# A fused attention and feed-forward kernel: 7 block products for tile 2 of the second layer, and tile 1 in the written order

## The chip, the cores and the metric

The kernel runs on one core of one Trainium2 chip. The metric is the device time of one launch in microseconds (us). The core has five engines that run side by side, each through its own queue in order: PE (TensorE, matmuls, with its weight loads as PEld), DVE (VectorE), ACT (ScalarE), POOL (GpSimd) and SP (SyncE, which here only issues transfers). PE writes to PSUM, of which this kernel uses eight banks of 2 KB per partition.

## The reference

Attention with separate softmaxes, for 8 batches of 8 heads, 576 positions and 64 channels, and then a feed-forward block on the 4608 x 512 result:

```python
q_s = softmax(q, axis=-1)                      # over the channels of a head
k_s = softmax(k, axis=2)                       # over the positions
kv  = einsum('bhsd,bhse->bhde', k_s, v)        # 64 x 64 per head
x   = einsum('bhsd,bhde->bhse', q_s, kv)       # then to (4608, 512)
h   = x @ w_in                                 # 512 -> 2048
out = maximum(0.01 * h, h) @ w_out             # 2048 -> 512
```

## The kernel before

**Tiles and batches.** The feed-forward block works on 9 tiles (0 to 8) of 512 rows. The attention works on 8 batches of 576 rows, so tile t needs rows of one or two batches: tile 1 the last 64 rows of batch 0 (their first layer is made with tile 0 and carried over) and the first 448 of batch 1, tile 2 the last 128 of batch 1 and the first 384 rows of batch 2, tile 3 the rest of batch 2 and the start of batch 3. While PE works on tile t, the other engines prepare the batch that a later tile needs.

**One batch.** k, q and v are loaded whole (1152 KB each, `load`, L76) into one of six buffers (`raw_pool`, bufs=6), a buffer being given on when its last reader is done. For k: a tree of maxima on DVE (`k_tree`, four steps kt.0 to kt.3), the maximum over all partitions (`k_allmax`, km), subtraction (`k_sub`, ks and ksB for the halves on DVE, or one step on POOL), exponential on ACT (`k_exp`, ke). For v: a cast to bf16 in two halves (`v_cast`, va and vb). For q: maximum on DVE (`q_max`, qm), subtraction on POOL (`q_sub`, qs), exponential on ACT (`q_exp`, qe), sum and reciprocal on DVE (`q_sum`, qu), scaling on DVE (`q_norm`, qn), and a transposition by a DMA that SP issues (`q_turn`, qt; the result is the tile qX). Then 72 small matmuls make the key-value products (`kv`, into two PSUM banks), these are divided by the sums of the keys (`kd_make`, L308, on DVE: reciprocal and multiplication, twice), and `attend_made` (A.0, A.1, A.2 in words) multiplies qX by them; the results go from PSUM to the tile xT by copies (x words, on ACT).

**One tile.** The first layer is 16 blocks of 4 matmuls of 128x128 weights by 512 columns (`layer1`, words u) into PSUM, each followed by a leaky rectifier on ACT (`leaky`, words l). The plain second layer is, for each of four groups of 128 rows, 16 matmuls of 512 columns into one bank (`layer2`, words P with two digits: group, quarter) and a copy out (words d0 to d3). From tile 3 on the second layer goes by 7 block products in Strassen's manner instead of 8 (`behind`, words P with three digits: product, group, half): each product is 16 matmuls of 256 columns, on sums of weight blocks (`wsums`, words T, made once) and differences of the rectified blocks (words n, on DVE); what stands in PSUM between products is kept by ACT (words q1, q5, q6, q21) and totalled by DVE (words d11, d12, d22). Tiles 7 and 8, and tile 6 in part, do the same with the first layer too (`ahead`, words m, s, c; the sums F1 to F4 of the first layer's weights are made for them by `fsums`).

**The order.** The scheduler leaves the program's order as it is, so every engine works through its part of one written list. Tiles 0 and 1 are loops over the 16 blocks and the 4 groups of rows, with hooks: `at(t, u, ...)` puts steps at a place u of tile t, and `run(t, u)` calls them (L510 to L517). Tile 1's loop is L1051 to L1064; its hooks are `plan2` and `plan3` (L614 to L637). From tile 2 on the order is a string of words, `SCORE` (L775), which `play` (L1042) reads word by word: a word with a leading digit is of that tile (`of_tile`, L914), the others are of a batch (`of_batch`, L985): `lk3` loads k of batch 3, `kt4.0` is the first step of batch 4's tree. `KS_DVE` (L718) lists the batches whose k is subtracted on DVE.

**SP's queue** around the change issues, in program order: tile 0's 8 stores, the loads k, q, v of batch 3 (`load_all(3)` at place 2 of tile 1), the two halves of batch 2's transposition (places 16 and 17), tile 1's stores, with the loads of batch 4 between them (place 30), and then what SCORE says.

**PE's order in tile 1** is: 16 blocks of the first layer; the second layer's first two groups of rows (32 matmuls); kv of batch 2; the third group and a quarter of the fourth (20 matmuls); the first part of batch 2's attention (5 of 9 columns of positions), 8 matmuls, the second part, 4 matmuls; then tile 2's first layer.

## Time and profile before

| what | us |
|---|---|
| median of 3 runs (271.74 to 271.83) | 271.76 |
| the profiled execution | 271.57 |
| its span, first to last instruction | 269.8 |
| PE busy in the span | 261.4 (97%) |
| DVE busy | 222.3 (82%) |
| ACT busy | 182.4 (68%) |
| POOL busy | 65.1 (24%) |
| granted clock of PE | 1.0 |

A busy PE is not a PE at its peak, because matmuls overlap: one of 512 columns is shown with 379 ns, while in a run of them one starts every 216 ns. So spans of PE work are read from the chain of work that ended last, which gives start, length and count of merged pieces. For the other engines the groups by line and shape give the mean time of one instruction: 602 ns for a leaky step of 512 columns on ACT, 419 ns for a difference (L954) and 687 ns for a total (L852) on DVE, 2.55 us for the maximum or the scaling of a whole q on DVE, 2.14 us for its exponential on ACT, 4.43 us for its subtraction on POOL, 1.36 us for half a k's subtraction on DVE, 292 and 163 ns for the two steps of `kd_make`. Tile 1 runs from 49.9 to 77.9 us, tile 2 from there to 107.2.

### The profile page before, as it was taken

The numbers are of one execution on the slowest core, as the hardware profiler recorded it, in microseconds if no ns is written. First come the engines' busy times: TensorE is split into PE (matmuls) and PEld (weight loads), VectorE is DVE, ScalarE is ACT, GpSimd is POOL, SyncE is SP. The second block draws the span as 40 slices with busy tenths as digits, with TensorE's granted clock in tenths as the row PEclk, the third lists the DMA queues.
The fourth block names the chain that finished last, engine by engine and source line by source line (L and its number), as shares of the span: only waits on it lengthen the run. The fifth ranks groups of instructions, "written<-read, shape, count | busy, mean of one in ns | idle before, by whom it ended". The sixth has DMA issues, their size and how long they took to land.

```text
span 269.8 us, 6101 instructions
## 1 busy us (share of the span) xinstructions
PE 261.4 (97%) x2474; PEld 179.2 (66%) x2474; DVE 222.3 (82%) x391; ACT 182.4 (68%) x328; POOL 65.1 (24%) x46
## 2 busy tenths in 40 slices
PE   8799999999999999999999999999999999999993
PEld 3267744454444444447888884488888888888882
DVE  2997888896897998999599869985999679769953
ACT  4977890578468846857587287839997579628930
POOL 2584351009007700001920290029000000000000
PEclk9999999999999999999999999999999999999999
DMA  7999996999999645079299609900393060024004
GB/s 247 337 211 367 306 204 103 383 326 389 175 248 400 227 87 177 0 161 365 75 318 305 149 5 286 229 0 2 75 183 70 2 156 2 0 59 99 4 0 156
DMA packets 37900, 46.46 MB, mean 172 GB/s; under 512 B 18160, under 2 KB 21232, under 8 KB 37872
## 3 DMA queue, kind: packets, MB, share of 16 engines
q1 hardware_dynamic: 33504, 37.82, 48.5%
q0 software_dynamic: 4048, 7.73, 12.1%
q10 hardware_dynamic: 320, 0.52, 0.6%
q8 instruction: 19, 0.31, 0.5%
q14 instruction: 9, 0.07, 0.1%
HBM read 36.70 MB, written 9.44 MB: 171 GB/s over the span
## 4 chain that ended last, share of the span: by engine, by line
PE 88%; DMA 5%; DVE 1%; issue 0%; POOL 0%; ACT 0%; POOLq 0%
PE ph L474 29%; PE acc L903 27%; PE pout L499 14%; PE ph L873 14%; DMA w_in_sb<-in_moe_w_in_dram 3%; PE po L419 2%; DMA qX<-qe 2%; PE pkv L294 2%; DVE k_raw L361 1%; POOL w_in_sb L129 0%; DVE out_sb L852 0%; ACT out_sb L493 0%; POOL gate L558 0%; POOLq L558 0%
## 5 line engine op out<-in xcount | busy, mean ns | idle before, releaser
L474 PE MATMUL ph<-xT,w_in_sb 128*128 128x256 bf16 (+3 forms) x512 | 86.0, 326 | 0.3 <-DMA w_in_sb<-in_moe_w_in_dram 0.2
L483 ACT ACTIVATE gj<-ph 128x512 bf16<-128x512 f32 (+2 forms) x116 | 61.6, 572 | 18.6 <-PE ph L474 15.9
L474 PEld LDWEIGHTS <-w_in_sb 128*128 128x128 bf16 x512 | 49.6, 98 | 33.7 <-issue 0.9
L499 PE MATMUL pout<-w_out_sb,gj 128*128 128x512 bf16 x192 | 43.1, 379 | 0.0
L256 POOL TENSOR_TENSOR q_raw<-q_raw,qmax 128x2304 f32<-128x2304 f32 (+3 forms) x10 | 31.6, 3165 | 38.9 <-DVE qmax L225 38.9
L903 PEld LDWEIGHTS <-gs 128*128 128x128 bf16 x384 | 37.0, 98 | 5.5 <-issue 0.8
L499 PEld LDWEIGHTS <-gj 128*128 128x128 bf16 x192 | 18.2, 98 | 22.0 <-issue 1.1
L193 POOL TENSOR_TENSOR k_raw<-k_raw,kall 128x2304 f32<-128x2304 f32 x3 | 15.4, 5137 | 68.5 <-DVE kall L185 51.5
L903 PEld LDWEIGHTS <-gj 128*128 128x128 bf16 x288 | 28.1, 98 | 3.9 <-issue 0.2
L410 ACT CAST xT<-po 128x320 bf16<-128x320 f32 (+2 forms) x45 | 18.5, 486 | 15.4 <-PE po L419 15.4
L852 DVE TENSOR_TENSOR part_spare<-ph,part_spare 128x512 f32<-128x512 f32 x36 | 23.7, 685 | 2.8 <-PE ph L873 2.5
L936 ACT COPY part_spare<-ph 128x512 f32<-128x512 f32 x36 | 19.3, 593 | 8.1 <-PE ph L873 7.8
L903 PE MATMUL acc<-w_out_sb,gj 128*128 128x256 bf16 x192 | 23.7, 273 | 0.0
L273 DVE TENSOR_REDUCE qsum<-qe 128x36 f32<-128x2304 bf16 (+4 forms) x11 | 19.7, 1794 | 4.6 <-ACT qe L264 4.6
L903 PE MATMUL acc<-wsum,gs 128*128 128x256 bf16 x192 | 23.3, 273 | 0.0
L903 PE MATMUL acc<-w_out_sb,gs 128*128 128x256 bf16 x192 | 22.3, 273 | 0.0
L280 DVE TENSOR_TENSOR qe<-qe,qrec 128x2304 bf16<-128x2304 bf16 (+4 forms) x12 | 21.9, 1826 | 0.4
L852 DVE TENSOR_TENSOR out_sb<-acc,keep 128x512 f32<-128x512 f32 (+1 forms) x20 | 12.5, 635 | 11.6 <-ACT xT L410 4.9
L225 DVE TENSOR_REDUCE qmax<-q_raw 128x36 f32<-128x2304 f32 (+4 forms) x11 | 19.6, 1794 | 2.2 <-DMA q_raw<-in_q_dram 2.2
L873 PEld LDWEIGHTS <-fs_spare 128*128 128x128 bf16 x192 | 18.8, 98 | 2.2
L954 DVE TENSOR_TENSOR gs<-gj,gs 128x512 bf16<-128x512 bf16 x48 | 19.5, 419 | 0.9
L954 DVE TENSOR_TENSOR gs<-gj 128x512 bf16<-128x512 bf16 x48 | 19.0, 419 | 0.9 <-ACT gj L483 0.8
(89 smaller groups left out, 324.0 us busy)
## 6 DMA issues: line engine op xcount, KB each, us to landing
out_dram<-out_sb SPq DMA_DIRECT2D x68, 128.0 KB, 2.5
k_raw<-in_k_dram SPq DMA_DIRECT2D x6, 1152.0 KB, 6.9
q_raw<-in_q_dram SPq DMA_DIRECT2D x6, 1152.0 KB, 7.2
...
```

Source lines behind the costliest of these rows:

```text
L225: nc.vector.tensor_reduce(out=m, in_=st[b]["q"][:, :, rs], axis=AX.X, op=ALU.max)
L256: eng.tensor_tensor(out=qs, in0=qs, in1=st[b]["qmax", rs.start].unsqueeze(3).to_broadcast([P, HL, n, D]), op=ALU.subtract,)
L273: nc.vector.reduce_sum(out=qsum, in_=st[b]["qe"][:, rs], axis=AX.X)
L280: nc.vector.tensor_tensor(out=qes, in0=qes, in1=st[b]["qrec", rs.start].unsqueeze(3).to_broadcast([P, n, HL, D]), op=ALU.mult,)
L474: nc.tensor.matmul(ph[:, n0:n1], lhsT=w_in_sb[:, i, j * P : (j + 1) * P], rhs=xT[:, i, (c0 + n0) % NX : (c0 + n0) % NX + n1 - n0], start=( ...
L483: nc.scalar.activation(out=o, in_=ph, func=AF.Prelu, alpha=LEAKY_SLOPE)
L499: nc.tensor.matmul(pout, lhsT=g_at(g_sb, j, tsub * P, (tsub + 1) * P), rhs=w_out_sb[:, j], start=first, stop=last,)
L852: nc.vector.tensor_tensor(out=o, in0=x, in1=y, op=ALU.add)
L873: nc.tensor.matmul(bank[x, t, p][:, jj], lhsT=lhs(k, 2 * p + jj), rhs=rhs[:, k], start=(first and k == 0 and jj == 0), stop=(k == 1), skip ...
L903: nc.tensor.matmul(b[:, at_], lhsT=lhs(k)[:, sub * P : (sub + 1) * P], rhs=rhs[:, k], start=(first and k == 0 and at_ == 0), stop=(k % (NK ...
L936: nc.scalar.copy(out=fill(t, kind, p), in_=bank["Z" if kind == "s5" else "X", t, p])
L954: nc.vector.tensor_tensor(out=nt[t, p, i], in0=x, in1=y, op=ALU.subtract)
```

## The change

Four things are done together.

1. Tile 2's second layer goes by the 7 block products too (words `2P100` to `2P711`, `2n`, `2q`, `2d11`, `2d12`, `2d22` in place of `2P00` to `2P33` and `2d0` to `2d3`). The weight sums T4 and T3 are therefore made in tile 2, T3 after tile 1's last plain product; the sums F1, F2 and F3 of the first layer's weights move from tile 2 into tiles 3 and 4.
2. Tile 1 and batch 2 become words of `SCORE`; the loop of tile 1 and `plan2`, `plan3` go. PE's order in tile 1 stays nearly the same (kv of batch 2 after the second group of rows, its first attention words after a quarter of the fourth group), only the second part of its attention comes half a group earlier. Batch 2's q is one piece in every step, its v is cast on ACT in place of POOL, and the loads come in another order: `lk3 lq4 lq3 lv3` before batch 2's transposition `qt2`, then `lq5 lv5 lk4 lv4 lk5`.
3. For batches 2 to 7 the division of the key-value products is split: `kr` makes both reciprocals on DVE, `kd` scales on ACT by four activations of 128x64 (`kd_scale`).
4. The rest of `SCORE` (tiles 3 to 6) is another order of the same words. Two options (`QS_DVE`, `QN_POOL`) are added and left empty.

```diff
+    def kd_recs(b):
+        st[b]["krec"] = []
+        for hh in range(2):
+            krec = small_pool.tile([P, 2, 1], FP32, name="krec")
+            nc.vector.reciprocal(out=krec, in_=st[b]["pkv"][hh][:, :, D : D + 1])
+            st[b]["krec"].append(krec)
+
+    def kd_scale(b):
+        for hh in range(2):
+            for i in range(2):
+                nc.scalar.activation(
+                    out=kd2[b % 2][:, 2 * hh + i],
+                    in_=st[b]["pkv"][hh][:, i, 0:D],
+                    func=AF.Copy,
+                    scale=st[b]["krec"][hh][:, i],
+                )
...
-    at(1, 2, lambda: load_all(3))
-    at(1, 30, lambda: load_all(4))
...
-    plan2()
-    plan3()
...
-    WOVEN, KS_DVE = 7, (3, 4)
+    WOVEN = 7
+    KS_DVE, QS_DVE, QN_POOL, KD_ACT = (2, 3, 4), (), (), (2, 3, 4, 5, 6, 7)
...
     SCORE = """
-        2u00 2u04 2l04 2u01 2l00 2l01 km3 ks3 2u02 2u03 2l02 2l03 qm3 2u06 2l06 2u13 2u17 2l13 ksB3 ke3 2l17
...
+        lk3 1u04 1l04 lq4 1u00 1u06 1l06 1l00 1u02 1u07 1l07 1l02 1u03 1u12 1l12 kt2.0 kt2.1 1l03 kt2.2 1u14
+        1l14 1u13 qm2 kt2.3 1u10 1l10 1l13 1u15 qs2 1u11 1l11 1u05 1l05 1u01 1l01 km2 1u16 1l15 qe2 1P00
+        1u17 ks2 1l17 1l16 va2 ksB2 qu2 qn2 1P01 1P02 1P03 1P10 1P11 lq3 1P12 kt3.0 lv3 1P13 ke2 vb2 kv2
+        kt3.1 kr2 1d0 1d1 kd2 qt2 1P20 1P21 1P22 kt3.2 kt3.3 1P23 1P30 A2.0 x2.01 x2.00 lq5 qm3 A2.1 A2.2
+        x2.20 1P31 1P32 x2.21 x2.11 qm4 km3 qs3 1d2 1P33 x2.10 2u04 2u02 1d3 qe3 lv5 2l04 2u15 2l15 qu3 2l02
+        qn3 qs4 va3 2u00 2l00 1w0 2u01 2l01 2u10 lk4 2u11 2u03 2u13 2l10 2l03 2u12 2l12 2P100 2l11 2l13 2u05
+        2l05 2n2_0 2u14 2l14 T4 2u06 2u16 2n0_0 1w1 2n1_0 2n0_1 vb3 ks3 2u17 2l06 2u07 2n1_1 2n2_1 2P200
+        2l16 2l17 ksB3 kt4.0 2l07 2P201 2n3_1 2n0_2 2n0_3 2n1_3 2P210 2P101 2P110 2P111 2P211 2P500 qt3
+        2n1_2 2n3_2 ke3 kv3 2q1 2P600 2P501 qe4 2d11 2n2_3 2P601 2P610 2P611 2n3_3 kr3 2P510 2n2_2 kd3 kt4.1
+        T3 A3.0 2q6 lv4 2n3_0 A3.1 x3.10 A3.2 x3.01 2P511 2P700 2P701 2P710 2P711 x3.00 kt4.2 kt4.3 km4 2q5
+        2P300 2P301 lk5 2d22 qu4 qn4 qt4 2P310 2P311 2d12 x3.20 x3.21 x3.11 3u06 2P400 2P401 ks4 2P410 va4
+        vb4 2P411 2q21 3l06 3u00 3l00 ksB4 3u04 3u10 3l10 3u05 3u17 3l04 3l05 kt5.0 2w0 3u02 3l02 lv6 3l17
...
-    t, c0 = 1, L
-    for u, j in enumerate(ORDER):
-        ph = psB_pool.tile([P, TT - c0], FP32, name="ph", tag=BANK_TAG)
-        layer1(j, ph, t * TT + c0, TT - c0)
-        leaky(g_at(g_next, j, c0, TT), ph)
-        run(t, u)
-    for tsub in range(NTS):
...
     play(SCORE)
```

More of the change, by code (lines that the diff above doesn't have):

```diff
@@ L275, in q_sum, with q_norm @@
         nc.vector.reciprocal(out=qrec, in_=qsum)
-    def q_norm(b, rs):
+    def q_norm(b, rs, eng=nc.vector):
         n = rs.stop - rs.start
         qes = st[b]["qe"][:, rs]
-        nc.vector.tensor_tensor(
+        eng.tensor_tensor(
             out=qes,
@@ L609 @@
         at(0, (45, 46)[i], lambda i=i: attend_x(1, (i,), (nc.scalar, nc.vector)))
-    at(1, 2, lambda: load_all(3))
-    at(1, 30, lambda: load_all(4))
-    def plan3():
-        b, t = 3, 1
-        at(t, 27, lambda: k_begin(b), lambda: k_tree(b, ALLH))
-        at(t, 26, lambda: v_cast(nc.scalar, b, 0), lambda: v_cast(nc.scalar, b, 1))
-    def plan2():
-        b = 2
-        at(1, 0, lambda: k_begin(b), lambda: q_begin(b), lambda: k_tree(b, ALLH))
-        at(1, 3, lambda: k_allmax(b))
-        at(1, 6, lambda: k_sub(nc.vector, b, H0), lambda: k_sub(nc.vector, b, H1))
-        at(1, 12, lambda: k_exp(b, ALLH))
-        for rs in XR:
-            at(1, 9, lambda rs=rs: q_max(b, rs), lambda rs=rs: q_sub(nc.gpsimd, b, rs))
-        at(1, 13, lambda: v_cast(nc.gpsimd, b, 0), lambda: v_cast(nc.gpsimd, b, 1))
-        for i, rs in enumerate(XR):
-            at(1, (15, 16)[i], lambda rs=rs: q_exp(b, rs), lambda rs=rs: q_sum(b, rs), lambda rs=rs: q_norm(b, rs))
-            at(1, (16, 17)[i], lambda rs=rs: q_turn(b, rs))
-        at(1, 23, lambda: kv(b))
-        at(1, 24, lambda: kd_make(b))
-        for i in range(2):
-            at(1, 28 + 2 * i, lambda i=i: attend_x(b, (i,), (nc.scalar,)))
-    plan2()
-    plan3()
     W11, W12 = w_out_sb[:, 0:NK, 0:HO], w_out_sb[:, 0:NK, HO:O]
@@ L775 @@
     SCORE = """
-        2u00 2u04 2l04 2u01 2l00 2l01 km3 ks3 2u02 2u03 2l02 2l03 qm3 2u06 2l06 2u13 2u17 2l13 ksB3 ke3 2l17
-        2u16 2l16 2u11 2l11 2u10 2l10 qm4 qs3 F3 kv3 kd3 2u07 2u05 lk5 qe3 2u12 2l05 2u14 2u15 2P00 qs4 qu3
-        2l12 2P01 2l14 2l15 2P02 2l07 2P03 2P10 2P11 qn3 2d0 F1 2P12 2P13 2P20 2P21 kt4.0 va4 qt3 2P22 2P23
-        T4 2d1 A3.0 vb4 A3.1 x3.10 A3.2 x3.01 kt4.1 kt4.2 F2 kt4.3 2d2 x3.20 km4 ks4 ksB4 2P30 2P31 x3.00
-        kt5.0 2P32 2P33 x3.11 x3.21 3u04 3u02 qe4 ke4 3u00 3l04 3u01 3l02 qu4 qn4 3u11 3l00 3u10 3l01 3u05
@@ L781 @@
-        kv4 kt5.1 kd4 3l11 kt5.2 3l10 3l05 3n0_0 lv5 T3 qt4 3u14 3l14 3u15 3l15 lq5 3u03 3n2_0 3u07 3u13
-        3u16 3l13 2d3 3l03 3n2_1 3n0_2 3u06 3l06 3l07 3u12 3l12 3P100 3u17 3l17 3P101 3n2_2 3P110 kt5.3 lk6
-        3n1_0 3n3_0 3n0_1 3n1_2 3n3_2 3P500 3n1_1 3l16 3P111 3q1 3n2_3 3n0_3 2w0 3n1_3 3n3_3 km5 2w1 A4.0
-        x4.00 A4.1 A4.2 x4.01 3P501 3P600 va5 x4.20 3P510 3n3_1 3P511 3q5 3P200 3P201 3P210 3P211 x4.21
-        3P601 3P610 3P611 3q6 3P300 3P301 ks5 3P310 3P311 qm5 x4.10 3P700 3P701 3P710 3P711 3d22 x4.11 4u03
@@ L786 @@
-        4u02 ke5 vb5 3P400 3P401 4l02 3P410 3d11 4l03 4u13 4l13 lv6 3d12 4u12 4l12 3P411 lk7 qs5 qe5 4u00
-        4u04 3q21 4u10 4u01 kt6.0 4l04 4l00 4l01 4l10 4n2_1 4u11 4l11 4u06 4u05 kt6.1 4l05 4n0_1 4u17 4l06
-        4l17 4n1_1 4n3_1 kt6.2 qu5 qn5 4u07 lq6 4n2_2 4u15 4l07 kt6.3 4l15 4n0_0 4n1_0 4n3_0 4n2_0 4u14 4l14
-        4n0_2 4n1_2 4u16 4l16 4P500 4P100 4P101 4P110 4P111 4P200 4P201 4P210 4P211 4n2_3 4q1 4P600 3w1
-        4n0_3 4P501 4n1_3 4n3_3 km6 4P510 4n3_2 kv5 4d11 va6 kd5 qt5 4P601 4P511 4P610 4q5 4P611 A5.0 4q6
@@ L791 @@
-        A5.1 A5.2 4P300 qm6 x5.00 4P700 4P701 4P710 4P711 4d22 4P301 4P310 4P311 4P400 4P401 4P410 x5.01
-        x5.10 x5.21 4P411 ks6 ke6 qs6 x5.20 x5.11 4d12 5u03 kt7.0 qe6 F4 kt7.1 5u14 5u02 5l02 5l03 5u04 qu6
-        qn6 5n2_1 5l04 5l14 5u05 5u12 5l12 5l05 kt7.2 vb6 5u01 5u00 5l00 5u13 5l13 5n0_1 5n1_1 5n3_1 5l01
-        5u06 5u10 3w0 5l06 5l10 5n2_2 5u11 5l11 lv7 kt7.3 5u16 5l16 lq7 4q21 5n2_0 5n0_0 5u15 5n1_0 4w0 5l15
-        5n3_0 5u07 5l07 5u17 5P500 5l17 5n0_2 5n1_2 5P100 5P101 5n3_2 5n2_3 5n0_3 5n1_3 km7 5P110 5P111 qt6
@@ L796 @@
-        5P200 5P201 5P210 5P211 5q1 5n3_3 5d11 5P501 kv6 va7 5P510 5P511 vb7 5q5 5P600 5P601 ks7 5P610 5P611
-        5q6 kd6 A6.0 x6.00 qm7 A6.1 x6.10 qs7 x6.11 A6.2 5P300 x6.21 5P700 5P701 5P710 5P711 5P301 5P310
-        x6.01 5P311 5d22 5P400 5P401 5P410 5P411 5d12 x6.20 X6.0 X6.1 ke7 kv7 qe7 X6.2 X6.3 Z0 5q21 5w1
-        6m1_0 kd7 6s1_0 6m5_0 6s5_0 6m1_1 6m5_1 6m1_2 Z1 qu7 6m6_0 6s1_1 6m2_1 6s6_0 6c11_1 6m1_3 6m6_1 Z2
-        6s1_2 6m2_0 6c11_0 6s5_1 6m7_0 6c22_0 5w0 6m3_0 6c12_0 6s1_3 6m6_3 6s6_1 6m7_1 6l11_0 6l11_1 6c22_1
@@ L801 @@
-        6l22_0 qn7 6m4_0 6m3_1 6m6_2 6m4_1 6l21_0 6m5_2 6m5_3 6m2_2 6c11_2 6s6_2 6m2_3 6c11_3 6l21_1 6P200
-        6s5_2 6m7_2 6c22_2 6s6_3 6m3_2 6m7_3 6P100 6s5_3 6l12_0 6l11_2 6l22_1 6l22_2 6m4_2 6c22_3 6l11_3
-        6l21_2 6m3_3 6n0_0 6n1_0 6m4_3 6P101 6P110 6l21_3 6P111 6c12_1 6P201 6P210 6l12_1 4w1 6P211 6c12_2
-        6l12_2 6l22_3 qt7 6c12_3 6l12_3 6n0_1 A7.0 A7.1 6n1_1 6n0_2 6n1_2 6P500 6n0_3 6n1_3 6q1 6P600 6P601
-        6P610 6n2_0 6P611 6q6 6n2_1 6P501 6P510 6P511 6n2_2 6n2_3 6P700 6P701 6P710 6d11 6P711 6q5 6n3_1
@@ L806 @@
-        6n3_0 6P300 6n3_3 6n3_2 x7.11 6P301 6P310 6d22 6P311 x7.00 x7.01 A7.2 x7.20 x7.10 6d12 6w0 x7.21
-        X7.0 6P400 6P401 X7.1 6P410 6P411 6q21 6w1 X7.2 X7.3
+        lk3 1u04 1l04 lq4 1u00 1u06 1l06 1l00 1u02 1u07 1l07 1l02 1u03 1u12 1l12 kt2.0 kt2.1 1l03 kt2.2 1u14
+        1l14 1u13 qm2 kt2.3 1u10 1l10 1l13 1u15 qs2 1u11 1l11 1u05 1l05 1u01 1l01 km2 1u16 1l15 qe2 1P00
+        1u17 ks2 1l17 1l16 va2 ksB2 qu2 qn2 1P01 1P02 1P03 1P10 1P11 lq3 1P12 kt3.0 lv3 1P13 ke2 vb2 kv2
+        kt3.1 kr2 1d0 1d1 kd2 qt2 1P20 1P21 1P22 kt3.2 kt3.3 1P23 1P30 A2.0 x2.01 x2.00 lq5 qm3 A2.1 A2.2
@@ new lines @@
+        T3 A3.0 2q6 lv4 2n3_0 A3.1 x3.10 A3.2 x3.01 2P511 2P700 2P701 2P710 2P711 x3.00 kt4.2 kt4.3 km4 2q5
+        2P300 2P301 lk5 2d22 qu4 qn4 qt4 2P310 2P311 2d12 x3.20 x3.21 x3.11 3u06 2P400 2P401 ks4 2P410 va4
+        vb4 2P411 2q21 3l06 3u00 3l00 ksB4 3u04 3u10 3l10 3u05 3u17 3l04 3l05 kt5.0 2w0 3u02 3l02 lv6 3l17
+        F1 3u03 3l03 3n2_1 3u01 3n2_2 3u15 3l01 kt5.1 kt5.2 kt5.3 ke4 3u13 3l13 3u11 3l11 3u12 3l15 3u14
+        3u07 3n0_0 3l12 3l14 3n0_2 3l07 3n1_2 kv4 3u16 3n0_1 va5 3P100 3P101 kr4 3n3_2 3n1_1 3P500 3P110
@@ new lines @@
+        3P111 3l16 3n2_0 3n2_3 kd4 A4.0 3n1_0 A4.1 A4.2 3n0_3 3P501 3n3_0 lk6 3P510 3P511 vb5 3q1 3P600
+        3n1_3 3P601 x4.00 lq6 3P200 x4.20 F2 3n3_3 3q5 3P610 3n3_1 x4.11 3P611 3q6 3P201 3P210 2w1 3P300
+        3P700 x4.01 3P701 3P710 3P711 qm5 km5 qs5 3d22 3P211 3d11 x4.21 x4.10 4u04 3P400 3P401 3P410 3P301
+        3P310 3P311 4l04 3P411 qe5 3d12 qu5 qn5 4u06 4l06 4u12 4u03 F3 F4 4u02 4l02 4l12 4l03 4u05 4u07 4l05
+        4u17 4u13 4u00 qt5 ks5 4u15 kt6.0 4l17 4l07 4l13 4n0_1 4n1_1 4u01 4n2_1 kt6.1 kt6.2 4l00 4n2_3 ke5
@@ new lines @@
+        4u11 4l15 4l11 4u10 kv5 4l10 kr5 4l01 4n0_0 lk7 3q21 3w1 kd5 4n1_0 4u16 4l16 4n2_0 4u14 4P100 4P101
+        4n3_0 4l14 4n0_2 A5.0 A5.1 A5.2 4P110 4P111 4P500 4n0_3 4P501 4P510 4q1 4n3_1 x5.21 x5.00 4P511 4q5
+        x5.11 4n1_2 4n1_3 4P600 4P601 4P610 4P611 4q6 kt6.3 4n3_3 4P300 4P200 4P201 4P700 4n2_2 4n3_2 4P301
+        4P310 x5.20 va6 qm6 x5.10 4P311 4P701 4P710 x5.01 qs6 4P711 km6 qe6 4P210 4P211 5u15 4d22 4P400 4d11
+        4d12 lv7 4P401 4P410 qu6 5u04 5l04 ks6 kt7.0 kt7.1 kt7.2 5u02 vb6 4P411 5u00 5l00 5l15 5u05 5l05 qn6
@@ new lines @@
+        5u13 5l02 qt6 5l13 5u14 5l14 5n0_2 5n1_2 lq7 ke6 5u03 5u11 5l11 5l03 kt7.3 5n2_1 5u10 5u12 5l12
+        5n0_1 5u01 5l01 5n2_2 5u07 5u06 5u16 5n2_0 5n1_1 5n3_1 5l10 5u17 5n0_0 5n1_0 5n3_0 4q21 5l06 5n3_2
+        5l07 5P100 5P101 5l16 5n2_3 5l17 5n0_3 km7 5n1_3 5P110 5P111 5q1 5P500 kv6 5P501 5P510 va7 5P600
+        5P601 5P610 kr6 kd6 5P611 A6.0 A6.1 A6.2 5q6 5P511 x6.00 ks7 5P700 3w0 5P200 5P701 5P710 qm7 qs7
+        5P711 x6.10 5P201 5q5 4w1 5n3_3 vb7 5P210 5P211 5d22 5P400 5P401 5P410 5P411 5P300 x6.11 ke7 x6.20
@@ new lines @@
+        5d11 4w0 5P301 5P310 x6.01 x6.21 X6.0 X6.1 X6.2 5q21 qe7 kv7 5P311 Z0 X6.3 6m1_0 6m5_0 6m1_2 kr7
+        5d12 6m1_1 kd7 qu7 Z1 6s1_0 6s1_2 6m2_2 6c11_2 6m6_0 6m1_3 6s1_1 Z2 6m5_2 6m2_0 6s6_0 5w0 6m7_0
+        6c11_0 6s5_0 6c22_0 6m6_2 6m2_1 6c11_1 6m6_1 6s5_2 6m3_0 6c12_0 6s1_3 6m6_3 6l11_2 6m4_0 6m2_3 6s6_2
+        qn7 6l11_0 6s6_1 6m7_1 6m7_2 6l11_1 6l21_0 6m5_1 6m5_3 5w1 6s6_3 6l22_0 6c11_3 6m7_3 6s5_1 6c22_1
+        6m3_2 6P100 6m3_1 6s5_3 6m3_3 qt7 6m4_1 6c22_2 6l12_0 6m4_2 6l11_3 6P101 6c22_3 6m4_3 6l22_1 6c12_2
@@ L808 @@
+        6c12_1 6P110 6c12_3 6l22_2 6P111 6l21_1 6l21_2 6P200 6n0_0 6l21_3 6P201 6P210 6P211 6n1_0 6l12_2
+        6n0_2 6n1_2 6l12_1 6n0_1 6n1_1 6l12_3 6l22_3 6n0_3 6n1_3 A7.0 A7.1 6q1 x7.11 6P500 6P600 6P601 6P610
+        6n3_0 x7.00 6P611 6P501 6P510 6P511 6n2_0 6q6 6n2_2 6n3_2 6n2_1 6P700 6n2_3 6P701 6P710 6P711 6n3_3
+        6q5 6n3_1 6d22 x7.01 6P300 6P301 6P310 6P311 6d11 6d12 6w0 A7.2 x7.21 x7.10 x7.20 X7.0 X7.1 X7.2
+        6P400 6P401 6P410 X7.3 6P411 6q21 6w1
     """.split()
@@ L818 @@
     """.split()
-    gt, nt, ot, bank, slots, free, made = {}, {}, {}, {}, {}, [], {}
+    gt = {(1, p): g for p, g in enumerate(g_next)}
+    nt, ot, bank, slots, free, made = {}, {}, {}, {}, [], {}
     SUB = {"n0": ("a2", "b2"), "n1": ("a1", "n0"), "n2": ("a2", "a1"), "n3": ("b1", "n1")}
@@ L919, in of_tile @@
             j = int(word[1]) * NK + p
-            bank["U", t, j] = psB_pool.tile([P, TT], FP32, name="ph", tag=BANK_TAG)
-            layer1(j, bank["U", t, j], t * TT, TT)
+            c0 = L if t == 1 else 0
+            bank["U", t, j] = psB_pool.tile([P, TT - c0], FP32, name="ph", tag=BANK_TAG)
+            layer1(j, bank["U", t, j], t * TT + c0, TT - c0)
         elif k0 == "l" and "_" not in word:
             h = int(word[1])
-            leaky(g_of(t, p // 2)[:, h, p % 2, 0:TT], bank["U", t, h * NK + p])
+            leaky(g_of(t, p // 2)[:, h, p % 2, L if t == 1 else 0 : TT], bank["U", t, h * NK + p])
         elif k0 == "m":
@@ L1011, in of_batch @@
         elif kind == "qs":
-            q_sub(nc.gpsimd, b, ALLR)
+            q_sub(nc.vector if b in QS_DVE else nc.gpsimd, b, ALLR)
         elif kind == "qe":
@@ L1018, in of_batch @@
         elif kind == "qn":
-            q_norm(b, ALLR)
+            q_norm(b, ALLR, nc.gpsimd if b in QN_POOL else nc.vector)
         elif kind == "qt":
@@ L1023, in of_batch @@
             kv(b)
+        elif kind == "kr":
+            kd_recs(b)
+        elif kind == "kd" and b in KD_ACT:
+            kd_scale(b)
         elif kind == "kd":
@@ L1049, in play @@
                 of_batch(word)
-    t, c0 = 1, L
-    for u, j in enumerate(ORDER):
-        ph = psB_pool.tile([P, TT - c0], FP32, name="ph", tag=BANK_TAG)
-        layer1(j, ph, t * TT + c0, TT - c0)
-        leaky(g_at(g_next, j, c0, TT), ph)
-        run(t, u)
-    for tsub in range(NTS):
-        po = psO_pool.tile([P, O], FP32, name="pout")
-        for i, j in enumerate(ORDER):
-            layer2(po, g_next, tsub, j, i == 0, i == NF - 1)
-            if i == NF - 1:
-                store(tsub, t * TT + tsub * P, po, nc.vector.tensor_copy if tsub == 2 else nc.scalar.copy)
-            if i % 4 == 3:
-                run(t, 16 + 4 * tsub + i // 4)
     play(SCORE)
```

## The prediction

> **What bounds the kernel now.** First the busy times of the page, then busy time by stage, to see which engine has no room where the change works.

> ```profile
> PE 261.4 (97%) x2474; PEld 179.2 (66%) x2474; DVE 222.3 (82%) x391; ACT 182.4 (68%) x328; POOL 65.1 (24%) x46
> ```
> ```profile
> 50.00:78.00 28.00, 27.79 (x217) 13.28 (x216) 23.85 (x40) 18.44 (x30) 6.37 (x4) 1.00 1.00 302
> 78.00:107.00 29.00, 29.00 (x216) 13.29 (x215) 25.58 (x33) 19.95 (x31) 10.00 (x2) 1.00 0.71 236
> 107.00:133.00 26.00, 26.00 (x251) 16.68 (x250) 22.19 (x40) 16.93 (x29) 5.76 (x2) 1.00 0.51 156
> ```

> The columns are stretch, length, then PE, PEld, DVE, ACT and POOL busy, clock, DMA share, GB/s. Tile 1 lies in the first row, tile 2 in the second: PE is full, DVE at 85% and 88%, and in tile 1 the DMA engines are full too (share 1.00). Then the chain of work that ended last:

> ```profile
> 61.99 6.92 PE pout L499 x32
> 68.91 0.02 issue
> ...
> 69.16 5.07 DMA qX<-qe
> 74.22 0.04 issue
> 74.26 0.47 PE po L419 x8
> ...
> 77.88 9.63 PE ph L474 x44
> ...
> 92.64 10.36 PE pout L499 x48
> ...
> 255.65 9.62 PE acc L903 x88
> ```

> From 23 to 265 us the chain is PE matmuls end to end, with one exception: the transposed queries of batch 2 (qX) come at 74.22, and PE, at its own work until about 73.9, waits 0.3 us for them. So a saving on PE counts in full if no input comes late, and the one input already a little late is qX of batch 2.

> **The change part by part.**

> *Tile 2's second layer.* Removed: 64 matmuls of 512 columns, by the chain 10.36/48 = 0.216 us each, 13.81 us. Added: 7 products x 16 matmuls of 256 columns at 9.62/88 = 0.1093 us, 12.24 us. **PE gains 1.57 us.** Spacing is the right measure, since the durations (379 and 273 ns) overlap. [...]

> DVE gains 16 differences (419 ns) and 3 totals (687 ns) and loses 2 copies (690 ns): +7.4 us. ScalarE gains 4 copies and loses 2, each 0.58 us: +1.2. Out of tile 2's stretch go three sums of first-layer weights (F1 to F3, 1.22 us each, now in tiles 3 and 4), T3 (1.22) comes in, and the products of batch 3 leave DVE (0.58). DVE thus has some 4.4 us more there, in a stage where it had 3.4 us of 29 idle; where that goes is followed below.

> *Products on ScalarE.* Per batch, DVE loses two multiplications (0.29 us) and ScalarE gets four activations of 128x64. No row shows that from PSUM; the nearest are 128x320 at 443 ns above and 128x1 at 206 ns below, a line through 128x320 and 128x512 gives 0.23 at 64 columns, and L238, the same shape with a sum, takes 334 ns. I take 0.25, so 1.0 us per batch, at most 1.3. The time from kv's end to the products goes from 0.9 to about 1.4 us. It is hidden where the products wait for qX anyway (batch 2), and has some 0.4 us to spare at batch 3 (below).

> *Tile 1 in the written order.* The same 64 + 64 matmuls in nearly the same PE order: kv of batch 2 still after 1P13, its first attention group still after 1P30. PE gets there at 49.88 + 16 x 0.757 + 13 x 0.863 + 0.71 = 73.9. The casts of v go from POOL to ScalarE (2 x 1.15 us), in ScalarE's waits there (1.9 us ahead of tile 1's second copy, 2.1 ahead of the moves); the second ends at 69.2, and kv starts 0.3 us late, hidden by qX.

> *q of batch 2 in one piece.* k2 lands at 51.5 and q2 at 54.4 as before. DVE: maximum 54.5 to 57.05; POOL subtracts in 4.05 to 4.2 (whole-q rows in quiet, and 2.33 + 1.87 here), until about 61.4; ScalarE's exponential 2.14, until 63.7. Ahead of the sum on DVE stand both subtractions of k2, which before were done ahead of the maximum. How they stand to POOL, two rows of batch 5 show:

> ```profile
> 132.31 4.05 POOL L256 TENSOR_TENSOR q_raw<-q_raw,qmax 128x2304 f32<-128x2304 f32 x1
> ```
> ```profile
> 134.90 2.54 DVE L160 TENSOR_TENSOR t<-k_raw 128x1024 f32<-128x1024 f32 x1
> ```

> The DVE step takes 1.22 us elsewhere; here it ends 1.1 us after POOL's end (136.36), as if it had stood until then. So k's subtractions run from 61.4 to 64.0, the sum and its reciprocal until 66.9, the scaling until 69.5, and the transposition is issued at about 69.6; its first half was issued at 69.16 before. [...]

> *The loads.* This is the step that decides. SP's queue, before:

> ```profile
> 58.32 0.53 SPq L83 DMA_DIRECT2D k_raw<-in_k_dram  x1
> 58.95 1.23 SPq L83 DMA_DIRECT2D q_raw<-in_q_dram  x1
> 60.28 0.45 SPq L83 DMA_DIRECT2D v_raw<-in_v_dram  x1
> 69.16 4.04 SPq L438 DMA_TRANSPOSE qX<-qe  x2
> ...
> 78.93 1.29 SPq L496 DMA_DIRECT2D out_dram<-out_sb  x2
> ```

> With their times to landing (5.7, 8.3, 9.9 us) the three loads are in at 64.0, 67.2 and 70.2, one per 3.1 us, and the transposition, issued at 69.16, had its way. In the new order **four** loads stand ahead of it: lk3, lq4, lq3, lv3. The fourth needs a buffer that falls free at the latest when q2's exponential ends (63.7), before the third has landed; so it lands at about 73.3. (q3, the third, is in before its maximum at 72.7; v3, the fourth, is cast at 84; lq5, lv5 and tile 1's stores come behind the transposition, and with three buffers no copy waits for those stores before tile 2's totals.) Does what follows in this queue wait for it? The stores issued at 78.93, right behind three loads:

> ```profile
> L496 SPq DMA_DIRECT2D out_dram<-out_sb x2: 602/624/646, 78.9 to 79.6; - x2
> ...
> DMA to landing us min/median/max: 9.9/10.1/10.3
> ```

> The same stores with nothing ahead land in 2.4 us: the queue is served in order. So the transposition starts at 73.3. Its own time is at least 2.47 us (its issue, batch 3) and at most 4.6 (issue to landing there); I take 3.2, nearer the lower end because its start-up passes while it stands in line. **qX lands at about 76.5 (75.8 to 77.9), 2.3 us later than before (74.22).** Behind it all of PE waits: A2.0, 1P31 and on; ScalarE's moves x2 and, behind those, batch 3's exponential.

> *After that.* From qX to tile 2's first matmul it took 77.88 - 74.26 = 3.6 us; in the new order the second attention group is issued earlier, and groups plus three blocks cost 0.81 + 2.59 = 3.4: 0.2 gained. Tile 2's first matmul is thus at 79.9, +2.1.

> *Tiles 2 to 6.* POOL's q3 step follows q3's maximum (72.7 to 75.2) and ends at 79.3; ScalarE then runs exponential, leakies, casts and ke3, q1, qe4, kd3 in line ahead of A3.0. Leaky 2l07 follows its matmul (94.1), then 0.6 + 2.12 + 0.58 + 2.14 + 1.0 gives 100.6, and PE comes to A3.0 at 79.9 + 21.1 = 101.0. It just fits. DVE has some 30 us of work against 26 of PE there, but what is late of it (2d12) only frees a bank needed in tile 3's second layer, 10 us on. The last two tiles are as before.

> **Sum**, against the profiled execution (271.57, of which 269.8 span): +2.3 - 0.2 - 1.57 = **+0.5**, 272.1. The median of the runs (271.76) is 0.2 above that execution: I predict 272.2.

> **Rivals.**

> *The queue doesn't hold qX (faster).* If the fourth load comes late enough or the transposition passes it, qX lands 4.6 us after 69.6, at 74.2, and PE doesn't wait. Then ScalarE is next: exponential of q3 at 79.4, and its line ends at 99.5, where PE would reach A3.0 at 98.9; 0.6 us of the gain goes. -0.2 - 1.57 + 0.6 = -1.1, 270.6 (269.9 to 271.2). [...] Against: the stores' 10.1 us.

> *ScalarE's line becomes the bound (slower).* kd3 stands behind ke3, q1 and qe4 (5.8 us in all), so A3.0 waits once anything in it is over 0.4 us later: k3's second subtraction on DVE late, or products at 0.33 each. The same pattern, products behind exponentials, comes again for batches 4 and 5. At 0.5 us each it adds 1.5: 273.7. For: ScalarE's work rises by some 9.5 us in all (6 x 1.0, 2.3, 1.2), DVE's lateness feeds it. Against: ScalarE was 68% busy, and leakies in a row are spaced 0.5 us, not 0.6.

> [...]

> **How the numbers follow.** Forecast 0.48 (own range 271.5 to 273.6, from qX at 75.8 to 77.9), faster rival 0.32, slower rival 0.20. A measurement of this kernel can tell about 0.2% (0.54 us) from no change. The forecast's range straddles that bound (272.3): 0.25 same and 0.23 slower. Faster 0.31, same 0.27, slower 0.42. The range leaves out a tenth on each side: 270.2 to 273.8.

> **What would show it.** Right: the chain of waits crosses to DMA qX with a landing near 76.5, four loads ahead of it in SP's queue, tile 2's first matmul near 80, and from there PE without gaps and tile 2 shorter by 1.6 us. Wrong: qX landing before 75, or the chain going through ScalarE's products (kd) or DVE between 95 and 135 us.

## The result, and the profile after

| | before | after |
|---|---|---|
| median of six runs, us | 271.75 (271.68 to 271.97) | 273.97 (272.44 to 274.24) |
| the profiled execution | 271.57 | 273.79 |
| its span | 269.8 | 271.7 |
| tile 2's first matmul | 77.88 | 81.53 |
| tile 7's first matmul | 216.35 | 218.26 |

The change makes the kernel slower: the ratio is 1.0072, with a 95% interval of 1.005 to 1.0095. The forecast was 272.2, slower the likeliest sign; the median lies 1.8 above the forecast and 0.2 above the upper end of the range (by the ratio, which goes by the means, 271.76 becomes 273.7, 0.1 inside it). Five of the six runs took 273.8 to 274.2, one took 272.44, and that difference has a cause of its own, below. (Line numbers have moved: L436 is the attention's matmul, L455 the transposition, L491 the first layer, L516 the plain second layer, L901 the block products.)

The busy times of the page, of the kernel after:

```profile
PE 260.4 (96%) x2522; PEld 184.1 (68%) x2522; DVE 225.5 (83%) x393; ACT 188.2 (69%) x354; POOL 61.0 (22%) x43
```

PE is busy 1.0 us less than before and yet the span is 1.9 us longer, so PE stands more. Where, the chain of work that ended last tells, of the kernel after. The columns are start, length, what:

```profile
69.43 7.04 DMA qX<-qe
...
76.52 0.92 PE po L436 x16
77.44 4.09 PE pout L516 x12
81.53 8.63 PE ph L491 x40
```

Before, this place read 74.22 for the landing of qX, 74.26 for the first attention group and 77.88 for tile 2's first matmul. So qX is 2.25 us later, and then something else happens: the three blocks left of tile 1, 12 matmuls of 512 columns, take 4.09 us, which is 0.341 each in place of 0.216. The waits of PE from 60 us on are one line, and it is the same wait:

```profile
PE po L436 <- DMA qX<-qe: 2.3, 1, 2.3
```

Busy time by stretch, of the kernel after, around that wait. The columns are stretch, length, then PE, PEld, DVE, ACT and POOL busy, granted clock of PE, DMA share, GB/s:

```profile
74.00:76.50 2.50, 0.18 (x1) 0.10 (x1) 2.50 (x2) 0.00 (x0) 1.75 (x1) 1.00 1.05 206
76.50:77.40 0.90, 0.89 (x17) 0.50 (x17) 0.90 (x2) 0.51 (x2) 0.90 (x1) 0.68 0.84 282
77.40:81.50 4.10, 4.10 (x16) 1.56 (x14) 2.25 (x9) 3.90 (x6) 4.10 (x2) 0.65 1.04 366
81.50:85.00 3.50, 3.50 (x18) 1.55 (x16) 3.40 (x3) 1.44 (x3) 1.31 (x1) 1.00 1.00 354
```

PE stands in the first row (0.18 us busy of 2.50), and in the two rows after it the granted clock is 0.68 and 0.65; from 81.5 on it is 1.00 again. So PE lost 2.3 us standing, and then it ran slowly: from 76.52 to 81.53 it took 5.01 us for the two attention groups and the 12 matmuls, for which the forecast had 3.4, so some 1.6 us more.

SP's queue, of the kernel after:

```profile
58.52 0.53 SPq L83 DMA_DIRECT2D k_raw<-in_k_dram  x1
59.15 1.81 SPq L83 DMA_DIRECT2D q_raw<-in_q_dram  x2
63.68 0.37 SPq L83 DMA_DIRECT2D v_raw<-in_v_dram  x1
69.43 5.06 SPq L455 DMA_TRANSPOSE qX<-qe  x1
```

Four loads stand ahead of the transposition. Before, there were three, and two half transpositions, issued at 69.16 and 71.7. When the fourth of them is in, the time to landing of v3's load tells, of the kernel after (the instructions on v_raw from 57 to 70 us):

```profile
DMA to landing us min/median/max: 10.8/10.8/10.8
```

Issued at 63.68, it lands at 74.5. SP's transposition instruction ends at the same time (69.43 + 5.06 = 74.49), and qX lands 2.0 us behind.

Batch 2's q on POOL and the two subtractions of its k on DVE, of the kernel after, from the timelines of the two engines:

```profile
57.26 4.16 POOL L256 TENSOR_TENSOR q_raw<-q_raw,qmax 128x2304 f32<-128x2304 f32 x1 [9.35 <-DVE qmax L225]
```
```profile
59.85 4.05 DVE L193 TENSOR_TENSOR k_raw<-k_raw,kall 128x1152 f32<-128x1152 f32 x2
```

The pair on DVE starts 1.6 us before POOL's end (61.42) and takes 4.05 us.

The end of ScalarE's line ahead of batch 3's attention, of the kernel after:

```profile
98.92 2.13 ACT L264 ACTIVATE qe<-q_raw 128x2304 bf16<-128x2304 f32 x1
100.95 0.92 ACT L330 ACTIVATE kd<-pkv,krec 128x64 bf16<-128x64 f32 x4
```

The four activations take 0.92 us in a row, one per 0.23. They end at 101.87 and PE comes to A3.0 at 102.71.

### The profile page after: what moved, and what is told of

Its sections match the earlier page's. It is cut to its first block, busy times and chain, and to the rows that moved or that the text cites. A ratio compares the mean times of both kernels' runs of the same rounds, so it can differ in the third digit from the quotient of the medians.

```text
span 271.7 us, 6210 instructions
## 1 busy us (share of the span) xinstructions
PE 260.4 (96%) x2522; PEld 184.1 (68%) x2522; DVE 225.5 (83%) x393; ACT 188.2 (69%) x354; POOL 61.0 (22%) x43
## 4 chain that ended last, share of the span: by engine, by line
PE 87%; DMA 6%; DVE 1%; issue 0%; POOL 0%; POOLq 0%
PE acc L901 32%; PE ph L491 29%; PE ph L871 14%; PE pout L516 9%; DMA w_in_sb<-in_moe_w_in_dram 3%; DMA qX<-qe 3%; PE po L436 2%; PE pkv L294 2%; DVE k_raw L378 1%; POOL w_in_sb L129 0%; DVE out_sb L850 0%; POOL gate L575 0%; POOLq L575 0%
## 5 line engine op out<-in xcount | busy, mean ns | idle before, releaser
L491 PE MATMUL ph<-xT,w_in_sb 128*128 128x256 bf16 (+3 forms) x512 | 86.4, 326 | 0.3 <-DMA w_in_sb<-in_moe_w_in_dram 0.2
L491 PEld LDWEIGHTS <-w_in_sb 128*128 128x128 bf16 x512 | 49.6, 98 | 33.1 <-issue 0.6
L256 POOL TENSOR_TENSOR q_raw<-q_raw,qmax 128x2304 f32<-128x2304 f32 (+3 forms) x9 | 29.8, 3317 | 98.5 <-DVE qmax L225 79.9
L901 PEld LDWEIGHTS <-gs 128*128 128x128 bf16 x448 | 43.2, 98 | 5.9 <-issue 0.6
L901 PEld LDWEIGHTS <-gj 128*128 128x128 bf16 x336 | 32.7, 98 | 5.7 <-issue 0.4
L516 PE MATMUL pout<-w_out_sb,gj 128*128 128x512 bf16 x128 | 30.4, 392 | 0.0
L901 PE MATMUL acc<-w_out_sb,gj 128*128 128x256 bf16 x224 | 28.5, 273 | 0.0
L953 DVE TENSOR_TENSOR gs<-gj 128x512 bf16<-128x512 bf16 x56 | 22.5, 419 | 6.3 <-ACT gj L500 6.2
L901 PE MATMUL acc<-wsum,gs 128*128 128x256 bf16 x224 | 27.0, 273 | 0.0
L901 PE MATMUL acc<-w_out_sb,gs 128*128 128x256 bf16 x224 | 26.7, 273 | 0.0
L953 DVE TENSOR_TENSOR gs<-gj,gs 128x512 bf16<-128x512 bf16 x56 | 24.7, 460 | 0.6
L516 PEld LDWEIGHTS <-gj 128*128 128x128 bf16 x128 | 12.4, 100 | 15.7 <-issue 2.7
L850 DVE TENSOR_TENSOR out_sb<-acc,keep 128x512 f32<-128x512 f32 (+1 forms) x23 | 14.4, 640 | 10.1 <-PE acc L901 6.8
L871 PE MATMUL ph<-xs_spare,fs_spare 128*128 128x256 bf16 x144 | 19.2, 273 | 0.0
```

The source lines that it names most:

```text
L256: eng.tensor_tensor(out=qs, in0=qs, in1=st[b]["qmax", rs.start].unsqueeze(3).to_broadcast([P, HL, n, D]), op=ALU.subtract,)
L491: nc.tensor.matmul(ph[:, n0:n1], lhsT=w_in_sb[:, i, j * P : (j + 1) * P], rhs=xT[:, i, (c0 + n0) % NX : (c0 + n0) % NX + n1 - n0], start=( ...
L516: nc.tensor.matmul(pout, lhsT=g_at(g_sb, j, tsub * P, (tsub + 1) * P), rhs=w_out_sb[:, j], start=first, stop=last,)
L850: nc.vector.tensor_tensor(out=o, in0=x, in1=y, op=ALU.add)
L871: nc.tensor.matmul(bank[x, t, p][:, jj], lhsT=lhs(k, 2 * p + jj), rhs=rhs[:, k], start=(first and k == 0 and jj == 0), stop=(k == 1), skip ...
L901: nc.tensor.matmul(b[:, at_], lhsT=lhs(k)[:, sub * P : (sub + 1) * P], rhs=rhs[:, k], start=(first and k == 0 and at_ == 0), stop=(k % (NK ...
```

## The experiments

**The loads, one fewer and one more ahead of the transposition.** The theory is that SP's queue sets the landing of qX. The first kernel takes the load of v3 out from ahead of it, the second puts a fifth load there.

```diff
 e1_v3_behind
-  lq3 1P12 kt3.0 lv3 1P13 ... kd2 qt2 1P20
+  lq3 1P12 kt3.0 1P13 ... kd2 qt2 lv3 1P20
 e3_five_loads
-  kd2 qt2 1P20 ... A2.0 x2.01 x2.00 lq5 qm3
+  kd2 lq5 qt2 1P20 ... A2.0 x2.01 x2.00 qm3
```

> The changed kernel with the load of v3 issued behind batch 2's transposition, so that three loads stand ahead of it in SP's queue. Queue theory (the transposition waits in line behind the fourth load, PE waits 2.3 us for it, and its clock falls after the wait): qX lands near 74.3, PE goes on at full clock, 270.4 to 270.8. Rival (the one-piece q or the products on ScalarE make batch 2 late, the queue does not matter): qX still lands after 76 and the time stays near 273.9.

Measured: 270.17 (270.0 to 270.91), ratio to the kernel before 0.9951 (0.9939 to 0.9963); repeated in another run as e1b_v3_behind, 270.42, 0.9953 (0.994 to 0.9966). With this one word moved the change is a gain. The chain of work of e1_v3_behind:

```profile
69.65 5.60 DMA qX<-qe
...
75.30 0.68 PE po L436 x16
75.98 2.70 PE pout L516 x12
```

The transposition is issued 0.2 us later than in the kernel after and lands 1.2 us earlier; the 12 matmuls take 2.70 us, and the granted clock stays at 1.00. It landed 1.0 us later than the 74.3 expected. That figure was the first half's landing in the kernel before; there the second half, issued at 71.7, landed 3.3 us later, at 75.0, and here PE waits for the one whole piece. This profiled execution was the slowest of its five runs (270.91); in the repeat qX came at 74.95.

> The changed kernel with the load of q5 issued ahead of batch 2's transposition as well, so that five loads stand ahead of it. Queue theory: one more load is 3.1 to 3.2 us, qX lands near 79.6, and the time is 276.9 to 277.4, if the clock falls once more for about as long. Rival (queue order does not matter): unchanged, 273.9.

Measured: 278.26 (277.62 to 278.61), ratio 1.0243 (1.0229 to 1.0256), qX at 80.48 after an issue at 69.69. The fifth load cost 4.0 us of landing, not 3.1, and the time is 0.9 us above the expected range. Busy time by stretch of e3_five_loads:

```profile
76.00:78.00 2.00, 0.00 (x0) 0.00 (x0) 1.97 (x3) 0.00 (x0) 2.00 (x1) 0.74 1.42 183
78.00:80.00 2.00, 0.00 (x0) 0.00 (x0) 1.86 (x8) 0.00 (x0) 2.00 (x2) 0.50 1.21 244
```

The clock falls while PE still stands: PE came to its wait at 74.3, and the granted clock goes from 1.00 to 0.50 at 77.0.

**The clock: work without use in the wait.** Ten matmuls on zeros ahead of batch 2's first attention group; the loads stay as in the kernel after.

```diff
 e2_fill
-  1P23 1P30 A2.0
+  1P23 1P30 W A2.0          # W: ten matmuls of 512 columns on a tile of zeros
```

> The changed kernel with ten idle matmuls of 512 columns on zeros put ahead of A2.0, 2.2 us of PE work in the place of the wait; nothing else is moved. Clock theory (the halved clock from 77 to 81 us follows from PE standing still for 2.3 us): qX still lands at 76.5, the granted clock stays at 1.0, and the time is 272.3 to 272.6, 1.5 less. Rival (the clock falls for another reason, or the lost time lies in the wait alone): 273.9 or more, with the same low clock.

Measured: 272.08 (271.68 to 273.84, 12 runs), ratio 1.0029 (1.0014 to 1.0044). The chain of e2_fill:

```profile
69.13 7.14 DMA qX<-qe
...
76.31 0.68 PE po L436 x16
77.00 2.70 PE pout L516 x12
```

qX lands nearly as late (76.27), PE does nothing useful in the wait, and yet 1.9 us are won, where 1.5 were expected: the 12 matmuls take 2.70 us at full clock. No execution has a mean clock under 0.997. Two of the twelve still took 273.6 and 273.8, with spans 1.7 and 1.9 us longer than the profiled one's; why is open. The wait and the slow stretch behind it are thus two separate costs.

**The queue alone, in the kernel before.** One load of batch 4 is issued before batch 2's transposition; nothing of the change is in it.

```diff
 e8_before_four_loads
-    at(1, 30, lambda: load_all(4))
+    at(1, 14, lambda: st[4].update(k=load(k, 4, "k_raw", [(ALLH, ALLR)])))
+    at(1, 30, lambda: load_rest(4))                 # q and v
```

> The kernel before with one step moved: k of batch 4 is loaded ahead of batch 2's transposition (place 14 of tile 1 instead of 30), so that four loads stand ahead of it in SP's queue in place of three. Nothing else of the change is in it. By the queue and the clock: the loads end at 64.0, 67.2, 70.2 and 73.3 us, the transposition starts behind the fourth and lands at 76.3 to 76.8 in place of 74.22, PE waits 2.3 to 2.6 us; that makes 273.9 to 274.2 in executions where the clock holds and 275.4 to 275.7 where it falls behind the wait. Rival, the queue does not hold the transposition and the changed kernel's late qX comes from its one piece and its order on the other engines: 271.4 to 271.9, qX at 74.2.

Measured: 273.61 (273.13 to 275.83), ratio 1.0079 (1.0053 to 1.0105), 1.7 us above the kernel before on that chip (271.87). The chain of e8_before_four_loads:

```profile
69.37 6.44 DMA qX<-qe
...
75.85 0.47 PE po L419 x8
```

The first half lands at 75.81 in place of 74.22. Direction and kind are as the queue has it; the landing is 0.5 us or more below the expectation, which took the whole transposition where PE needs the first half to begin (the second half, issued at 72.0, landed 4.7 us later, in the range expected for the whole). The rival (qX at 74.2) is out.

**The issue, later.** Batch 2's q is subtracted on DVE, with POOL idle; the loads stay as in the kernel after.

```diff
 e10_q_on_dve
-    KS_DVE, QS_DVE, QN_POOL, KD_ACT = (2, 3, 4), (), (), (2, 3, 4, 5, 6, 7)
+    KS_DVE, QS_DVE, QN_POOL, KD_ACT = (2, 3, 4), (2,), (), (2, 3, 4, 5, 6, 7)
```

> The changed kernel with one option set: q of batch 2 is subtracted on DVE (one step of 2.6 us, by twice the 1.27 us that half a k's subtraction takes) in place of POOL (4.2 us). q2's exponential then ends near 61.8, the two subtractions of k2 run with nothing beside them on POOL and end near 62.5, and the transposition is issued near 68.0 in place of 69.43; the loads stay as in the changed kernel, four of them ahead. My theory, the queue sets the landing: qX lands at 76.2 to 76.6 all the same, the wait of PE stays at 2.1 to 2.4 us and the time within 0.6 of the changed kernel on the same chip (273.6 to 274.5 with the clock's fall, 272.4 without). [...]

The expected issue was wrong: the steps of k's maximum over all partitions stand behind q's subtraction on DVE (2.3 us that were forgotten), so the transposition is issued 1.2 us later than in the kernel after, not 1.4 earlier. That makes the test no weaker. The timeline of DVE and the chain of e10_q_on_dve:

```profile
62.50 2.63 DVE L193 TENSOR_TENSOR k_raw<-k_raw,kall 128x1152 f32<-128x1152 f32 x2
```
```profile
70.66 5.92 DMA qX<-qe
...
76.62 0.76 PE po L436 x16
77.38 4.26 PE pout L516 x12
```

Issued at 70.66 in place of 69.43, qX lands at 76.58 in place of 76.47: 1.2 us of the issue change the landing by 0.1. The load of v3 landed at 74.6 here, and qX again 2.0 us behind it. The time is 274.6 (272.72 to 276.73), ratio 1.0114 (1.0076 to 1.0153), not told apart from that of the kernel after. And with POOL idle the two subtractions of k take 2.63 us, against 4.05 beside POOL.

**Real work in the wait.** Blocks of tile 1's second layer move ahead of the first attention group: two of them with the loads as in the kernel after, and one with v3 behind the transposition as in e1_v3_behind.

```diff
 e11_blocks_ahead
-  1P23 1P30 A2.0 ... A2.1 A2.2 x2.20 1P31 1P32 x2.21
+  1P23 1P30 1P31 1P32 A2.0 ... A2.1 A2.2 x2.20 x2.21
 e7_block_ahead (on e1_v3_behind)
-  1P23 1P30 A2.0 ... x2.20 1P31 1P32 x2.21
+  1P23 1P30 1P31 A2.0 ... x2.20 1P32 x2.21
```

> The changed kernel with eight matmuls (1P31 and 1P32, 1.73 us) ahead of the first attention group of batch 2 instead of behind it; the loads are untouched, so qX lands at 76.3 to 76.5 as before. PE's wait falls from 2.3 to 0.6 us, and the moves to xT (2.4 us from 76.8) then end at 79.2, so tile 2's first matmul comes at about 79.3. My theory, the wait costs its length and the clock's fall behind it: the clock stays at 1.00, and the time is 271.7 (271.3 to 272.0), 2.2 us under the changed kernel. Rival, the clock falls for another reason than the wait: 273.2 or over.

Measured: 272.0 (271.42 to 273.36, 12 runs), ratio 1.0015 (1.0001 to 1.0028), 2 us under the kernel after. The profiled execution is the slowest of the twelve, and shows why. Chain of e11_blocks_ahead:

```profile
69.45 8.27 DMA qX<-qe
...
77.76 0.68 PE po L436 x16
78.44 1.45 PE pout L516 x4
```

In that one execution qX came 1.3 us later than expected, PE waited 2.0 us after all, and the four matmuls behind took 0.36 us each: the clock fell (mean 0.991). In the other eleven the mean is 0.996 or more.

> The changed kernel with v of batch 3 behind the transposition (as in e1_v3_behind, 270.17), and the four matmuls 1P31 ahead of the first attention group of batch 2 instead of behind it. In e1_v3_behind PE stands 1.0 us for qX; the 0.86 us of 1P31 would lie in that wait. The moves to xT on ScalarE (six, 2.4 us from 75.7) end at 78.1, and tile 2's first matmul, at 78.68 in e1_v3_behind, would be ready at 77.85, so the moves take 0.2 to 0.3 of it. My theory: 0.55 us won, 269.6 (269.4 to 269.8), PE's wait for qX under 0.3 us. Rival, what is won here is lost to the next engine (DVE or ScalarE in tile 2): within 0.2 of 270.17.

Measured: 270.47 (269.78 to 271.76), ratio 0.9955 (0.9939 to 0.9971), where e1_v3_behind had 0.9951: 0.9 us above the forecast, and 0.1 us above the rival's range too. The two ran again, side by side on one chip:

> e7_block_ahead again, beside e1b_v3_behind on the same chip. In the two profiles tile 2's first matmul comes 0.9 us earlier with 1P31 ahead, and the last instruction too, so the median should be 0.4 to 0.9 us lower than that of e1b_v3_behind. Rival, the two are the same within 0.2 us, and the wait of 1.0 us in e1_v3_behind was not in every execution.

> e1_v3_behind again, beside e7b_block_ahead on the same chip: 270.2 (269.9 to 270.6).

Measured: e7b_block_ahead 270.52 (0.9955, 0.9941 to 0.997), e1b_v3_behind 270.42 (0.9953): the same, as the rival had it. PE's wait is gone in the profiles of e7_block_ahead, but 0.5 us did not come. Over both tests the median span is 267.95 us against 268.15, so 0.2 us are won in the span; the rest went to what lies around the span, which was 3.0 to 3.7 us in six of the fourteen executions with the block ahead, and in one of ten without. Why is open.

**What the block products bring alone.** e1_v3_behind with tile 2's second layer plain again.

```diff
 e5_tile2_plain (on e1_v3_behind)
-  2P100 ... 2P200 ... 2q1 2P600 ... 2q6 ... 2d22 ... 2P411 2q21
+  2P00 ... 2P03 2P10 ... 2d0 ... 2d1 ... 2d2 ... 2P33 T3 2d3    # 16 words P, no n
```

> The changed kernel with v of batch 3 behind the transposition (as in e1_v3_behind, 270.17), and tile 2's second layer plain again: 64 matmuls of 512 columns and four copies in place of the 7 products, their differences and totals; the weight sum T3 is made after the last plain product. All else as in e1_v3_behind. My theory, PE paces tile 2 and nothing else comes late: the price is 64 x 0.216 - 112 x 0.1093 = 1.57 us, so 271.7 (271.4 to 272.0), and tile 2's stretch is 1.6 us longer with its start unmoved. Rival, the 16 differences and three totals on DVE delay something behind and eat part of the saving: then the plain form costs less than 0.8 us more, 270.9 or under.

Measured: 272.0 (271.47 to 272.91), ratio 1.0008 (0.9999 to 1.0017); against e1_v3_behind's 0.9951 that is 0.0057, or 1.5 us. In the profiles tile 2's first matmul comes at 78.77 and 78.68, and the last stretch of tile 3's first layer (56 matmuls) begins at 108.80 and 107.11: the plain form takes 1.60 us more. This is the forecast's 1.57, and nothing of it is lost behind: the spans differ by 1.7 us. The two lines of the chain, e5_tile2_plain first and then e1_v3_behind:

```profile
108.80 12.09 PE ph L491 x56
```
```profile
107.11 12.09 PE ph L491 x56
```

**The products, on DVE again.** Once in the kernel after, once in e1_v3_behind.

```diff
 e4_kd_on_dve, e6_kd_on_dve (on e1_v3_behind)
-    ..., KD_ACT = (2, 3, 4), (), (), (2, 3, 4, 5, 6, 7)
+    ..., KD_ACT = (2, 3, 4), (), (), ()             # and kr does nothing
```

> The changed kernel with the key-value products of all batches divided on DVE as before (reciprocal and multiplication in place of the words kd, no words kr). Queue theory: PE waits for qX at 76.5 as before, the time stays within 0.4 of 273.9. Rival (the products on ScalarE delay the attention or the leaky steps): 1 us or more is won.

Measured: 273.82 (271.63 to 275.56, 12 runs), ratio 1.0069 (1.0043 to 1.0096), the same as the kernel after. The twelve runs fall apart into six with a mean clock of 0.992 to 0.994 (274.0 to 275.6) and six without (271.6 to 273.6); the profiled one, with the wait of 2.4 us, is of the latter.

> The changed kernel with v of batch 3 behind the transposition (as in e1_v3_behind, 270.17), and the division of the key-value products of batches 2 to 7 on DVE again in one step (0.9 us per batch in place of 1.0 on ScalarE after two reciprocals). My theory, neither line is late anywhere once the wait for qX is short: within 0.3 of e1_v3_behind, 269.9 to 270.5. Rival 1, the products on ScalarE hold its line back ahead of A3.0, A4.0 or A5.0: with them gone 0.5 us or more is won, 269.7 or under. Rival 2, DVE is the engine short of time and ScalarE the right place: 0.5 us or more is lost, 270.7 or over.

Measured: 271.03 (270.77 to 271.4), ratio 0.997 (0.9961 to 0.998), by the ratios about 0.5 us above e1_v3_behind: rival 2, at its edge. One place of it shows in the profile, a wait of PE in tile 6's first layer:

```profile
PE ph L871 <- DVE part_spare L850: 0.2, 1, 0.2
```

The chain of e6_kd_on_dve comes to it through batch 6's division on DVE (190.7 to 191.5), and from 188.7 to the next stretch of first layer it takes 0.36 us longer than e1_v3_behind. The rest of the 0.5 us isn't located. So in this order of words the scaling on ScalarE is a small gain at batch 6.

## Why the prediction was right in sign and short in size

Forecast and measurement step by step, both against the execution profiled before:

| step | forecast | measured |
|---|---|---|
| transposition issued | 69.6 | 69.43 |
| the fourth load lands | 73.3 | 74.5 |
| from there to qX's landing | 3.2 | 2.0 |
| qX lands | 76.5 | 76.47 |
| PE starts the attention later by | 2.3 | 2.26 |
| qX to tile 2's first matmul, against 3.62 before | 3.4 (-0.2) | 5.01 (+1.39) |
| tile 2's first matmul | 79.9 | 81.53 |
| won from there to tile 7 | 1.57 | 1.74 |
| around the span | 0 | +0.3 |
| sum | +0.5 | +2.2 |

*The loads.* Right in place and cause; the landing itself came out by luck, since two terms were off by 1.2 us each and cancel. The fourth load landed at 74.5 and not at 73.3, and the transposition took 2.0 us from there and not 3.2. That a start-up passes while the transposition stands in line, which the 3.2 was chosen by, was my estimate; no run shows it. From the end of SP's transposition instruction, which in the kernel after is when the last load lands, to qX's landing it is 1.9 to 2.1 us in the profiles with four or five loads ahead (after, e2, e3, e4 and e10). Nor is the fourth load the whole of the 2.25 us. Without it, in e1 and e1b, qX still lands 0.7 to 1.0 us later than before, as one piece where PE before needed only the first of two; the load itself is worth 1.2 to 1.5. The forecast, which put all of it on the load, and the faster rival's 74.2 overlooked this.

The rival in which the queue doesn't hold qX is excluded by three runs: moving one load from ahead brought the landing down by 1.2 us with a later issue, the same step in the kernel before cost 1.7 us, and an issue 1.2 us later changed the landing by 0.1. All these transfers are on SP's queue; a load on another queue was not run. In the traces qX lands 2.0 us behind the last load, whether issued at 69.43 (after) or at 70.66 (e10_q_on_dve).

*The failed term.* "Groups plus three blocks cost 0.81 + 2.59 = 3.4: 0.2 gained" took PE at its full clock directly behind a wait. It took 5.01, because the clock fell (0.68 and 0.65 in the two stretches behind the wait). With the clock held it took 3.38, in e2_fill and in e1_v3_behind, so the sum of the work was right. e2_fill as a whole came to a ratio of 1.0029, or 0.8 us above the kernel before, where the forecast's sum has 0.5; the one run of the kernel after at a clock of 1.0 took 272.44. The fall is 1.6 us in the profiled execution, nearly all of the 1.8 by which the median lies above the forecast. I had read the clock only in the stretches of before, where it is 1.00 and PE never stands for over 0.3 us, and put no price on what the new wait does to it.

A small slip stands beside it: the sum gives 271.76 + 0.53 = 272.3 for the median, and not 272.2.

*The block products.* 1.57 us forecast, 1.60 in the profiles of e5_tile2_plain against e1_v3_behind. The 1.74 of the table has the rest of the new order in it.

*ScalarE's line.* 0.25 us each was taken, 0.23 measured; it was ready 0.84 us before A3.0 where 0.4 was forecast (0.84 in e2_fill too, at full clock), so the slower rival did not come about. ScalarE's busy time rose by 5.8 us, where 9.5 were forecast. The forecast gave the move to ScalarE no gain of its own: with the products back on DVE, e6_kd_on_dve loses some 0.4 us at batch 6. The kernel before, with its products on DVE, has no such wait of PE.

*DVE's load.* The forecast had some 30 us of work for DVE in tile 2, against 26 of PE. From 81.5 to 107.4 it was busy 23.3 of 25.9 us, and the extra work lay in tile 1 (29.1 from 50 to 81.5 us, against 23.85 from 50 to 78 before). Nothing on the chain came late by it.

*DVE beside POOL.* k's two subtractions were forecast to run from 61.4 to 64.0, and ended at 63.9. That POOL's subtraction beside them made them long is shown by e10_q_on_dve: 2.63 us with POOL idle, against 4.05 in the kernel after.

*Around the span.* The profiled time less its span is 1.8 us before and 2.1 after. In every execution but a few it is 1.8 in the versions with 328 to 352 instructions on ScalarE (before, e4, e5, e6, e8) and at least 2.1 in those with 354 (after, e1, e2, e3, e7, e10, e11). What it is was not tested, and 0.3 us of the result stay without a cause.
